# Three blocks on one core: whole-row loads of the key windows, the v-means spread from the load queue, and a new list of steps

## The chip, the core and the metric

The kernel runs on one core of a Trainium2 chip. Its engines work side by side, each through its own list in order: TensorE (PE, with its weight loads PEld), VectorE (DVE), ScalarE (ACT), GpSimd (POOL) and SyncE (SP), which here only issues transfers. The metric is device time in microseconds; of several runs the median counts.

## The reference

Three blocks follow one another. Attention: for 2 batches of 8 heads (768 positions, 64 wide) every query sees the keys within 16 positions and 24 summary keys, each the maximum over a block of 32 keys; the summary values are the means of v over the same blocks.

```
scores_l = scale * np.matmul(q, k.transpose(0, 1, 3, 2))          # kept where |i - j| < 16
scores_s = scale * np.einsum('bhsd,bhnd->bhsn', q, k.reshape(B, H, nb, block, D).max(axis=3)) + np.log(block)
a = softmax(concat([masked scores_l, scores_s]));  out = a @ concat([v, v.mean per block])
```

Then a mixing block: `u = x + (x^T @ U @ V)^T` (rank 32) and `u + relu(u @ w_ch1) @ w_ch2` (512 to 2048 and back), and last a block that shifts by one position: `sigmoid(xr @ w_r) * (relu(xk @ w_k)**2 @ w_v)`. All in float32; the large products run as three products of rounded high and low parts.

## The kernel before, in words

The kernel has a first stage, whose order is written out by hand, and a rest, which is generated by loops. The first stage holds the attention of all eight pairs of heads (numbered 0 to 7; 0 to 3 are batch 0), the rank-32 mixing, and the first quarter of the 2048 hidden units for batch 0. The string ORDER lists its steps by short names; a loop at the end of `build` calls the function of each step, and each step appends its instructions to the engines they belong to. So ORDER sets every engine's own order, and that of the load queue; nothing else moves. Semaphores wait for data and for buffers.

For a pair n of heads, cut into 3 groups g: LK, LQ, LT, LV, LW load keys, queries, v transposed, v in windows (`vcat`), and, for pairs 4 to 7 only, the keys cut into 12 overlapping windows (`kw`, built on GpSimd by KK for pairs 1 to 3). K and SV reduce keys and v by blocks on VectorE, KS writes the 24 block maxima behind each of the 12 windows, SP turns the sums of v on TensorE, VM writes their means from ScalarE, and SPR spreads these means to 12 places in `vcat`. S is the scores (TensorE), X adds the mask (VectorE), E is the exponential (ScalarE), T the transpose (TensorE), C its copy (ScalarE), V the product with the values (TensorE), N the division (VectorE). G, H, U with their copies GC, HC, HS, UC, UL are the rank-32 mixing. F, R, L, Z, Y are the first quarter of the hidden layer. The steps cl, ca, cb, cc, cs, cg, cp, ch, co load a block of weights (two small ones, 0 and 1, then eight of 512 KB) and round it into parts: load; ScalarE (ca, cb); VectorE (cc, cs, cg); GpSimd (cp); ScalarE (ch); GpSimd or VectorE (co).

The raw blocks lie in three staging buffers `stg`, of which blocks 0, 3, 6 and 9 share one: cl9 waits for the step cg6 on VectorE. There are three buffers for keys (`kt`, pair n in n mod 3), three for queries, and two each for `kw`, `vcat` and v transposed. All loads go through the one queue of SyncE; a load that waits for its buffer holds up those behind it. `vcat` has 120 rows of keys, 96 from the window and 24 means, so step V of a pair needs both LV and SPR.

In `spread` (line 208) the means go by GpSimd for pairs 0 to 3, and for 4 to 7 by two transfers, one for each head, issued by ScalarE (line 214). `load_kw` (line 174) writes 96 of each 120 columns of `kw`: 12 pieces of 384 bytes in each of 128 partitions. Behind the first stage come the loads of two small vectors (`muk`, `mur`) and of the next blocks of weights, on the same queue.

Of the kernel before, what the change touches and what calls it, by code (L numbers as in the profile page):

```python
# [42 lines left out]


ORDER = """
LK0 LQ0 cl0 LT0 LK1 LT1 LQ1 cl1 K0 S0.0 S0.1 X0.0 ca0 E0.0 X0.1 TV0.1 S0.2 E0.1 SV0 KK1 LK3 T0.0 K1 TC0.1 SP0
VM0 X0.2 KS1 LK4 E0.2 LK2 SPR0 LQ2 S1.0 LV1 SV1 TV0.2 cb0 TV0.0 X1.0 cb1 T0.1 LT2 TC0.0 S1.2 C0.1 cc1 LT3 S1.1
TC0.2 cg0 V0.1 C0.0 cc0 cs0 cl3 E1.0 KK2 V0.0 K2 SP1 ca1 X1.1 T0.2 cp0 VM1 C0.2 T1.0 X1.2 ch0 KS2 V0.2 SPR1
C1.0 S2.1 N0.0 LV2 E1.2 LK5 LQ3 SV2 KK3 V1.0 E1.1 X2.1 LT4 cl2 T1.2 S2.0 C1.2 N0.2 T1.1 E2.1 N0.1 V1.2 cg1
X2.0 G0 ca3 S2.2 GC0 C1.1 cs1 SP2 T2.1 K3 LW4 E2.0 cp1 LQ4 H0 V1.1 X2.2 VM2 KS3 ch1 LV3 T2.0 HC0 N1.0 C2.1 co1  # L50
S3.1 HS0 E2.2 N1.1 U0.1 SPR2 N1.2 cb2 S3.0 X3.1 C2.0 G1 co0 UC0.1 S3.2 X3.0 E3.0 V2.0 T2.2 SV3 GC1 U0.0 C2.2
X3.2 V2.1 E3.1 V2.2 SV4 SP3 LV4 H1 VM3 cl5 T3.0 ca2 N2.0 SPR3 LQ5 SP4 LT5 N2.1 HC1 C3.0 LW5 T3.1 HS1 E3.2 N2.2
U1.0 cg2 G2 C3.1 cc2 V3.0 cl4 UC0.0 cs2 LQ6 T3.2 VM4 UL0.1 cp2 GC2 U1.1 UC1.0 K4 C3.2 H2 V3.1 HC2 N3.0 YM0
UC1.1 KS4 V3.2 ch2 HS2 UL1.0 U2.0 cb3 co2 S4.1 cb5 N3.2 N3.1 S4.0 SPR4 UL0.0 G3 UL1.1 U2.1 X4.1 F1.0.0 UC2.0
GC3 F1.0.1 E4.1 cg3 F0.0.0 cc3 H3 UC2.1 cs3 F0.0.1 UL2.0 HC3 cp3 ca5 T4.1 HS3 F0.0.2 UL2.1 C4.1 U3.1 X4.0 ch3
U3.0 E4.0 co3 S4.2 SV5 F1.0.2 cb4 X4.2 LT7 T4.0 LK7 ca4 F0.1.0 LT6 C4.0 F0.1.1 cg5 UC3.0 F0.1.2 cc5 cl7 UC3.1
UL3.0 cl6 E4.2 V4.1 LK6 cs5 V4.0 LW6 UL3.1 cp5 LV5 SP5 K5 F0.0.3 VM5 F0.1.3 N4.0 R0.0 KS5 F1.1.0 ch5 N4.1
F1.0.3 SPR5 cg4 F1.1.1 cc4 cl8 co5 S5.0 R1.0 T4.2 L0.0 R0.1 F1.1.2 cs4 cb7 X5.0 F0.2.0 cp4 E5.0 F0.2.1 L1.0
F1.2.0 C4.2 L0.1 F1.2.1 ca7 K6 S5.1 S5.2 cc7 KS6 T5.0 X5.1 E5.1 F1.2.2 F0.2.2 cg7 F1.2.3 C5.0 X5.2 F1.1.3 R1.2
T5.1 R1.1 cs7 V4.2 E5.2 L1.1 cp7 V5.0 N4.2 S6.0 C5.1 L1.2 F0.2.3 ch4 X6.0 T5.2 ch7 co4 G4 C5.2 N5.0 S6.1 ca6  # L60
co7 S6.2 cb6 cg6 V5.1 GC4 E6.0 V5.2 X6.1 cl9 F1.3.0 LV7 E6.1 F1.3.1 LV6 cc6 LQ7 N5.2 F1.3.2 LW7 R0.2 cs6
F0.3.0 SV7 cp6 F0.3.1 F0.3.2 SV6 F0.3.3 ch6 X6.2 F1.3.3 cb8 co6 T6.1 ca8 Z1.0.2 N5.1 C6.1 T6.0 L0.2 SP6 cc8
C6.0 G5 cs8 ca9 SP7 cg8 Z0.0.3 E6.2 K7 Z0.1.3 cp8 Z0.0.2 cb9 Z0.1.2 VM7 Z1.1.2 ch8 cg9 cc9 Z0.0.1 VM6 co8 GC5
cs9 SPR6 Z0.1.1 Z0.0.0 Z0.1.0 KS7 R0.3 H4 cp9 Z0.2.1 R1.3 L0.3 Z0.2.2 L1.3 Z1.2.2 ch9 Z0.2.0 HC4 co9 HS4 S7.1
Z0.2.3 X7.1 Z0.3.3 Z1.3.2 Z0.3.2 Y1.2 H5 Y0.2 Z0.3.1 HC5 E7.1 Y0.3 S7.2 HS5 S7.0 X7.2 SPR7 V6.1 V6.0 Y0.1 T6.2
Z0.3.0 X7.0 U4.1 E7.0 U4.0 N6.0 Z1.0.1 E7.2 N6.1 T7.0 Z1.1.1 UC4.0 Z1.2.1 C6.2 UL4.0 U5.0 C7.0 Y0.0 Z1.3.1
UC5.0 V6.2 V7.0 N6.2 U5.1 UL5.0 T7.1 N7.0 T7.2 C7.1 Y1.1 UC4.1 C7.2 V7.1 V7.2 N7.1 Z1.0.0 N7.2 G6 UL4.1 G7 GC6
Z1.1.0 GC7 H6 Z1.2.0 HC6 UC5.1 H7 HS6 Z1.0.3 HC7 Z1.1.3 HS7 U7.0 U6.0 UC7.0 Z1.2.3 UC6.0 U7.1 UL6.0 Z1.3.0
UL7.0 U6.1 UC6.1 UC7.1 UL6.1 UL7.1 Z1.3.3 Y1.3 UL5.1 Y1.0
"""  # L70
# [808 lines left out]
```

## Time and profile before

| | us |
|---|---|
| median of 3 runs (lowest, highest) | 526.6 (524.32, 528.57) |
| the profiled execution, own time | 525.12 |
| its span | 523.3 |
| PE / DVE / ACT / POOL busy in the span | 505.9 / 319.8 / 250.5 / 195.2 |
| matmuls of the first stage | 5.0 to 114.0 |

The span runs from the first to the last instruction; the 1.8 us around it are start and end. The page's busy time of PE says little about waits by itself, because matmuls overlap and their ends are modelled; the timeline, with the idle time before each instruction, shows them. PEclk is the clock granted to TensorE, as a share of 2.4 GHz. From 114 us on TensorE runs the loops.

### The profile page before, as it was taken

To read this page: it belongs to the slowest core of one execution; us is meant where nothing else is said; L and a number is where in the kernel's file an instruction comes from. 1 tells how busy PE (TensorE), PEld (TensorE's weight loads), DVE (VectorE), ACT (ScalarE), POOL (GpSimd) and SP (SyncE) were. 2 spreads that over 40 slices of the span, in tenths; PEclk is the share of its full clock that TensorE was granted. 3 is DMA by queue.
4 is the path that set the end of the run, shared out by engine and by line. 5 is a ranking of instruction groups with operands and counts; after the bars stand their busy time and mean duration, and the time that the engine had idled before them with its cause. 6 is when DMAs were issued, how large, how long until landed. Compare 5 with 4: busy or idle time off the path is not lost.

```text
span 523.3 us, 8909 instructions
## 1 busy us (share of the span) xinstructions
PE 505.9 (97%) x3468; PEld 469.7 (90%) x3468; DVE 319.8 (61%) x702; ACT 250.5 (48%) x532; POOL 195.2 (37%) x176
## 2 busy tenths in 40 slices
PE   5799989999999999999999999999999999999997
PEld 4578869899999999999999999999879889889885
DVE  5689866646764788738876477556867424443212
ACT  4798676434523545334543445334585534532211
POOL 5544225004653777637776363160622110120000
PEclk9799989999999999999999999999999999999999
DMA  8898939102332333313333150040201001000101
GB/s 293 278 269 267 278 96 249 39 1 81 121 85 76 99 109 117 120 41 120 103 110 110 51 152 3 1 120 5 76 1 60 1 1 60 2 1 20 41 0 60
DMA packets 23737, 48.66 MB, mean 93 GB/s; under 512 B 11264, under 2 KB 11520, under 8 KB 23696
## 3 DMA queue, kind: packets, MB, share of 16 engines
q1 hardware_dynamic: 21120, 47.28, 29.7%
q10 hardware_dynamic: 2544, 0.77, 0.7%
q8 instruction: 27, 0.44, 0.3%
q14 instruction: 14, 0.11, 0.1%
q0 software_dynamic: 32, 0.05, 0.0%
HBM read 44.36 MB, written 3.15 MB: 91 GB/s over the span
## 4 chain that ended last, share of the span: by engine, by line
PE 87%; DMA 4%; ACT 3%; DVE 2%; POOL 1%; issue 1%; SPq 1%; DVEq 0%; POOLq 0%; ACTq 0%
PE bank L511 22%; PE bank L484 22%; PE bank L663 13%; PE bank L685 12%; PE bank L647 5%; DMA kt<-kt 4%; PE bank L579 3%; PE bank L290 2%; PE bank L274 2%; PE bank L555 2%; PE bank L245 2%; PE bank L343 1%; PE bank L312 1%; ACT P L268 1%; PE bank L347 1%
## 5 line engine op out<-in xcount | busy, mean ns | idle before, releaser
L408 POOL TENSOR_TENSOR A<-C,A 128x512 int32<-128x512 int32 (+1 forms) x54 | 70.8, 1311 | 115.9 <-DVE A L402 90.7
L444 POOL TENSOR_TENSOR wlo<-A,whi 128x512 fp32r<-128x512 f32 x50 | 71.1, 1421 | 37.1 <-ACT whi L440 34.7
L511 PE MATMUL bank<-hh,whi 128*128 128x384 f32 x224 | 76.0, 339 | 0.5 <-DVE y L523 0.5
L511 PE MATMUL bank<-hl,whi 128*128 128x384 f32 x224 | 75.7, 338 | 0.0
L511 PE MATMUL bank<-hh,wlo 128*128 128x384 f32 x224 | 75.7, 338 | 0.0
L484 PE MATMUL bank<-uhi,whi 128*128 128x384 f32 x224 | 75.4, 337 | 0.0
L484 PE MATMUL bank<-uhi,wlo 128*128 128x384 f32 x224 | 75.4, 336 | 0.0
L484 PE MATMUL bank<-ulo,whi 128*128 128x384 f32 x224 | 75.4, 336 | 0.0
L491 DVE SCALAR_TENSOR_TENSOR hl<-bank,hh 128x384 fp32r<-128x384 f32 x56 | 31.1, 556 | 68.3 <-ACT hh L489 68.2
L667 DVE TENSOR_TENSOR kt<-kt 128x384 f32<-128x384 f32 x32 | 20.4, 637 | 64.9 <-ACT kt L666 64.8
L385 ACT ACTIVATE A<-stg 128x512 f32<-128x512 uint32 (+1 forms) x54 | 36.3, 673 | 41.9 <-DMA stg<-w 21.6
L489 ACT ACTIVATE hh<-bank 128x384 fp32r<-128x384 f32 x56 | 27.3, 488 | 58.0 <-PE bank L484 57.8
L440 ACT CAST whi<-A 128x512 fp32r<-128x512 f32 x52 | 32.2, 622 | 37.7 <-POOL A L408 37.5
L402 DVE SCALAR_TENSOR_TENSOR A<-stg,A 128x512 int32<-128x512 int32 (+1 forms) x54 | 49.2, 912 | 1.4 <-ACT A L385 1.4
L398 DVE TENSOR_SCALAR C<-C 128x512 int32<-128x512 int32 (+1 forms) x54 | 44.2, 819 | 1.7
L663 PE MATMUL bank<-xkl,whi 128*128 128x384 f32 x128 | 43.2, 338 | 0.6 <-POOL xkl L625 0.6
L511 PEld LDWEIGHTS bank<-hh,whi 128*128 128x128 f32 x224 | 42.0, 188 | 1.5 <-ACT C L388 0.8
L663 PE MATMUL bank<-xkh,whi 128*128 128x384 f32 x128 | 43.2, 337 | 0.0
L663 PE MATMUL bank<-xkh,wlo 128*128 128x384 f32 x128 | 43.1, 337 | 0.0
L484 PEld LDWEIGHTS bank<-ulo,whi 128*128 128x128 f32 x224 | 42.1, 188 | 0.0
L484 PEld LDWEIGHTS bank<-uhi,wlo 128*128 128x128 f32 x224 | 42.1, 188 | 0.0
L511 PEld LDWEIGHTS bank<-hh,wlo 128*128 128x128 f32 x224 | 42.1, 188 | 0.0
(119 smaller groups left out, 1082.6 us busy)
## 6 DMA issues: line engine op xcount, KB each, us to landing
stg<-w SPq DMA_DIRECT2D x32, 512.0 KB, 4.0
stg<-wk SPq DMA_DIRECT2D x8, 512.0 KB, 3.6
stg<-wv SPq DMA_DIRECT2D x8, 512.0 KB, 3.7
vcat<-vw SPq DMA_DIRECT2D x7, 585.0 KB, 10.4
kt<-kt SPq DMA_DIRECT2D x8, 384.0 KB, 6.3
vt<-vt SPq DMA_DIRECT2D x8, 384.0 KB, 6.0
out<-sig SPq DMA_DIRECT2D x12, 256.0 KB, 2.1
qt<-qt SPq DMA_DIRECT2D x7, 384.0 KB, 8.7
```

Of the source, the lines that this page charges most:

```text
L385: nc_s.activation(tmp(i, "A"), st[i]["raw"][:, :, 0].bitcast(U32), AF.Copy, scale=2.0 ** -51, bias=2.0)
L398: nc_v.tensor_scalar(out=c, in0=c, scalar1=3, scalar2=None, op0=ALU.logical_shift_left)
L402: nc_v.scalar_tensor_tensor(out=a, in0=st[i]["raw"][:, :, 1], scalar=-2 ** 31, in1=a, op0=ALU.bitwise_and, op1=ALU.bitwise_or)
L408: nc_p.tensor_tensor(out=a, in0=c, in1=a, op=ALU.add)
L440: nc_s.copy(wt[key][0], w)
L444: eng.tensor_tensor(out=lo, in0=w, in1=hi.bitcast(F32), op=ALU.subtract)
L484: nc_t.matmul(ps, w[:, sl], x[:, k], start=(n == 0), stop=(n == 3 * KD - 1))
L489: nc_s.activation(hh, ps, AF.Relu)
L491: lambda: nc_v.scalar_tensor_tensor(out=hl, in0=ps, scalar=0.0, in1=hh.bitcast(F32), op0=ALU.max, op1=ALU.subtract)
L511: nc_t.matmul(acc[d], w[:, sl], x, start=(i == 0 and n == 0), stop=(i == FT - 1 and n == 2))
L663: nc_t.matmul(ps, w[:, sl], x[:, k], start=(n == 0), stop=(n == 3 * KD - 1))
L685: nc_t.matmul(acc, x[:, sl], w, start=(f == 0 and n == 0), stop=(f == KFT - 1 and n == 2))
```

## The change

`kw` of batch 1 is loaded with its full width of 120 columns: the array in memory gets 24 columns of zeros behind each window, and each partition is one piece of 5760 bytes. KS writes the maxima over these zeros, and so now waits for the load. The means of v get a third dimension with a column of ones (filled once), so that the 130 values of a place in `vcat` are written in one run; for pairs 4 to 7 SPR is one transfer, and SyncE issues it, in the queue of the loads. ORDER is a new list of the same 526 steps. The rest is unchanged.

```
 ORDER = """
-LK0 LQ0 cl0 LT0 LK1 LT1 LQ1 cl1 K0 S0.0 S0.1 X0.0 ca0 E0.0 X0.1 TV0.1 S0.2 E0.1 SV0 KK1 LK3 T0.0 K1 TC0.1 SP0
...
+LK0 LQ0 LK1 LT0 cl0 K0 S0.0 X0.0 S0.1 TV0.0 S0.2 E0.0 T0.0 TV0.1 TV0.2 X0.1 K1 X0.2 SV0 LK2 K2 E0.1 ca0 cb0
...
+SV1 S1.1 S1.0 S1.2 X1.0 T0.2 V0.0 V0.1 SP1 ca1 cb1 E1.0 cc0 X1.1 cg1 N0.0 cs0 C0.2 VM1 E1.1 N0.1 X1.2 E1.2 SV2
...
+    vm_b = [a_p.tile([128, 2, D + 1], F32, name=f"vm{i}", bufs=1) for i in range(2)]
+    for vc, vm in zip(vcat, vm_b):
...
+        nc_p.memset(vm[KW:KC], 1.0)
...
     def load_kw(n):
-        nc.sync.dma_start(out=kw_b[n % 2][:, :, 0:KW], in_=I["kw"][n - 4])
+        nc.sync.dma_start(out=kw_b[n % 2], in_=I["kw"][n - 4])
...
     def v_mean(n):
         held = ps_t.pop(("SP", n))
-        vm = vm_t[n] = a_p.tile([128, 2, D], F32, name="vm", bufs=2)
         nc_s.activation(
-            vm[KW:KC].rearrange("p h d -> p (h d)"), held[0][KW:KC, 0:2 * D], AF.Copy, scale=1.0 / BLK
+            vm_b[n % 2][KW:KC, :, 0:D], held[0][KW:KC, 0:2 * D].rearrange("p (h d) -> p h d", h=2), AF.Copy,
+            scale=1.0 / BLK,
         )
...
     def spread(n):
-        src = vm_t.pop(n)[KW:KC].unsqueeze(1).to_broadcast([NB, NT, 2, D])
+        src = vm_b[n % 2][KW:KC].rearrange("p h d -> p (h d)").unsqueeze(1).to_broadcast([NB, NT, 2 * (D + 1)])
+        dst = vcat[n % 2][KW:KC].rearrange("p t h d -> p t (h d)")
         if n < 4:
-            nc_p.tensor_copy(vcat[n % 2][KW:KC, :, :, 0:D], src)
+            nc_p.tensor_copy(dst, src)
         else:
-            for h in range(2):
-                nc_s.dma_start(out=vcat[n % 2][KW:KC, :, h, 0:D], in_=src[:, :, h])
+            nc.sync.dma_start(out=dst, in_=src)
...
-    ar["kw"] = kp[:, :, win]
+    ar["kw"] = np.concatenate([kp[:, :, win], np.zeros((4, 2 * D, NT, NB), np.float32)], axis=-1)
```

Three places show how the list moves work. The first is the load queue (SyncE) from its fourth transfer on; kt_110, kt_111 and kt_112 are the three key buffers, so kt_112 takes the keys of pair 2. Before, and then in the change:

```order
L376 DMA stg<-uva 128x1024
L169 DMA vt_113<-vt 128x768
L159 DMA kt_111<-kt 128x768
L169 DMA vt_114<-vt 128x768
L166 DMA qt<-qt 128x768
L376 DMA stg<-vb 96x896
L159 DMA kt_110<-kt 128x768
L159 DMA kt_111<-kt 128x768
L159 DMA kt_112<-kt 128x768
L166 DMA qt<-qt 128x768
L172 DMA vcat_105<-vw 96x1560
```

```order
L161 DMA kt_111<-kt 128x768
L171 DMA vt_113<-vt 128x768
L378 DMA stg<-uva 128x1024
L161 DMA kt_112<-kt 128x768
L171 DMA vt_114<-vt 128x768
L168 DMA qt<-qt 128x768 x2
L378 DMA stg<-vb 96x896
L168 DMA qt<-qt 128x768
```

The keys of pair 2 were the twelfth transfer, behind the keys of pairs 3 and 4; they are now the seventh.

The second is the same queue further on, around the loads for pair 5: its window of values is the first `vcat_105<-vw` below, and `vcat<-vm` is a spread of means. Before, and then in the change:

```order
L159 DMA kt_111<-kt 128x768
L169 DMA vt_113<-vt 128x768
L376 DMA stg<-w 128x1024 x2
L159 DMA kt_110<-kt 128x768
L175 DMA kw_108<-kw 128x12x96
L172 DMA vcat_105<-vw 96x1560
L376 DMA stg<-w 128x1024 x2
L172 DMA vcat_105<-vw 96x1560
```

```order
L177 DMA kw_109<-kw 128x1440
L174 DMA vcat_105<-vw 96x1560
L216 DMA vcat_104<-vm_125 24x12x130
L174 DMA vcat_104<-vw 96x1560
L161 DMA kt_111<-kt 128x768
L177 DMA kw_108<-kw 128x1440
L378 DMA stg<-w 128x1024
L161 DMA kt_110<-kt 128x768
L171 DMA vt_113<-vt 128x768
L171 DMA vt_114<-vt 128x768
L177 DMA kw_109<-kw 128x1440
L216 DMA vcat_105<-vm_126 24x12x130
```

The values of pair 5 stood behind the keys and windows of pair 6 (kt_110, kw_108) and two blocks of weights; they now stand ahead of all of pair 6. The spread of pair 5 (the last row) stands in this queue, behind the windows of keys of pair 7 (the second kw_109).

The third is ScalarE in pair 5. L268 before and L270 in the change are exponentials, L279 and L281 the copies C, L385 and L387 the first step on a block of weights (ca). Before, and then in the change:

```order
L562 ACTIVATE hh_1202<-bank_1132 128x384
L562 ACTIVATE hh_1210<-bank_1062 128x384
L268 ACTIVATE P<-P,nm 128x120 x4
L279 COPY pt_106<-bank_1205 120x512
L440 CAST whi<-A 128x512 x2
L279 COPY pt_107<-bank_1265 120x512
L385 ACTIVATE A<-stg 128x512
L388 ACTIVATE C<-stg 128x512
L317 COPY g_1321<-bank_1274 128x128
```

```order
L270 ACTIVATE P<-P,nm 128x120 x4
L442 CAST whi<-A 128x512
L387 ACTIVATE A<-stg 128x512
L281 COPY pt_107<-bank_1314 120x512
L442 CAST whi<-A 128x512
L390 ACTIVATE C<-stg 128x512 x2
L270 ACTIVATE P<-P,nm 128x120 x4
L387 ACTIVATE A<-stg 128x512
```

In the change the first step on weight block 8 stands between the exponentials of the last group of pair 5 and the copy that its product V5.2 waits for; the first exponentials of pair 6 follow behind. Before, it came after that copy.

## Rows read from the trace of the kernel before

**Rows 1.** Stretches: span, busy PE, PEld, DVE, ACT, POOL (counts), PEclk, DMA share, GB/s.

```profile
21.10:27.20 6.10, 6.07 (x73) 4.72 (x73) 4.72 (x26) 4.27 (x13) 3.97 (x5) 0.52 0.71 212
45.00:50.00 5.00, 5.00 (x66) 4.53 (x66) 4.81 (x19) 3.45 (x11) 1.79 (x2) 1.00 1.12 334
67.90:70.40 2.50, 0.00 (x0) 0.01 (x1) 1.54 (x4) 2.50 (x8) 1.54 (x2) 1.00 0.37 113
70.40:77.00 6.60, 6.58 (x116) 5.19 (x116) 3.80 (x21) 3.14 (x10) 0.99 (x1) 0.74 0.07 8
...
114.00:523.30 409.30, 404.35 (x2161) 383.20 (x2159) 240.53 (x375) 175.03 (x331) 155.34 (x120) 1.00 0.20 62
```

**Rows 2.** Timeline of TensorE: start, us, instruction, count, [idle before, releaser].

```profile
18.17 0.65 PE L274 MATMUL bank<-ident,P 128*120 128x128 f32 x4
21.13 1.08 PE L274 MATMUL bank<-ident,P 128*120 128x128 f32 x4 [2.31 <-DVE nm L257]
...
63.07 1.05 PE L245 MATMUL bank<-kw,qt 64*64 64x120 f32 x32
...
67.18 0.69 PE L290 MATMUL bank<-vcat,pt 121*64 121x65 f32 x16
70.42 0.69 PE L290 MATMUL bank<-vcat,pt 121*64 121x65 f32 x16 [2.56 <-ACT whi L440]
...
75.84 1.15 PE L290 MATMUL bank<-vcat,pt 121*64 121x65 f32 x32
```

**Rows 3.** Timeline of VectorE around two reductions of keys.

```profile
19.43 0.95 DVE L180 TENSOR_REDUCE ks<-kt 128x24 f32<-128x768 f32 x1 [2.50 <-DMA kt<-kt]
...
63.91 0.95 DVE L180 TENSOR_REDUCE ks<-kt 128x24 f32<-128x768 f32 x1 [1.90 <-DMA kt<-kt]
```

**Rows 4.** Timeline of the load queue on SyncE, transfers issued.

```profile
10.55 1.33 SPq L159 DMA_DIRECT2D kt<-kt  x3
...
29.66 0.65 SPq L175 DMA_DIRECT2D kw<-kw  x1
30.36 1.91 SPq L166 DMA_DIRECT2D qt<-qt  x1
...
55.36 0.55 SPq L175 DMA_DIRECT2D kw<-kw  x1
55.95 4.31 SPq L172 DMA_DIRECT2D vcat<-vw  x1
60.37 15.94 SPq L376 DMA_DIRECT2D stg<-w  x2
77.04 0.80 SPq L172 DMA_DIRECT2D vcat<-vw  x2
...
78.98 3.98 SPq L787 DMA_DIRECT2D muk<-moe_mu_k  x1
```

**Rows 5.** Timeline of ScalarE, with the issues of its own queue (ACTq).

```profile
13.94 1.17 ACT L388 ACTIVATE C<-stg 128x512 f32<-128x512 f32 x2
...
23.09 2.40 ACT L268 ACTIVATE P<-P,nm 128x120 f32<-128x120 f32 x8
...
45.12 1.41 ACTq L214 DMA_DIRECT2D vcat<-vm  x1
...
46.58 0.79 ACTq L214 DMA_DIRECT2D vcat<-vm  x1
...
68.96 0.57 ACT L279 COPY pt<-bank 120x512 f32<-120x512 f32 x1
```

**Rows 6.** DMA issues by tile: queue, count, size of one, median us to landing.

```profile
vcat<-vw SPq DMA_DIRECT2D x7, 585.0 KB, 10.4
...
kw<-kw SPq DMA_DIRECT2D x4, 576.0 KB, 8.7
```

**Rows 7.** Landing times of the weight blocks in the first stage (tile view).

```profile
DMA to landing us min/median/max: 4.3/5.8/11.1
```

**Rows 8.** Timeline of GpSimd: one spread of head pair 0.

```profile
12.88 1.47 POOL L211 COPY vcat<-vm 24x1536 f32<-24x1536 f32 x1 [1.79 <-ACT vm L203]
```

More of the change, by code (lines that the diff above doesn't have):

```diff
@@ L45 @@
 ORDER = """
-LK0 LQ0 cl0 LT0 LK1 LT1 LQ1 cl1 K0 S0.0 S0.1 X0.0 ca0 E0.0 X0.1 TV0.1 S0.2 E0.1 SV0 KK1 LK3 T0.0 K1 TC0.1 SP0
[L47 to L69, printed above, removed]
+LK0 LQ0 LK1 LT0 cl0 K0 S0.0 X0.0 S0.1 TV0.0 S0.2 E0.0 T0.0 TV0.1 TV0.2 X0.1 K1 X0.2 SV0 LK2 K2 E0.1 ca0 cb0
+TC0.0 T0.1 SP0 TC0.1 E0.2 VM0 C0.1 C0.0 TC0.2 KK1 KK2 KS1 LT1 LQ1 LQ3 cl1 LQ2 LV1 LT2 cl2 cl3 LK3 KS2 SPR0 cg0
@@ new lines @@
+SV1 S1.1 S1.0 S1.2 X1.0 T0.2 V0.0 V0.1 SP1 ca1 cb1 E1.0 cc0 X1.1 cg1 N0.0 cs0 C0.2 VM1 E1.1 N0.1 X1.2 E1.2 SV2
+cp0 SPR1 YM0 KK3 V0.2 N0.2 S2.0 T1.0 C1.0 T1.1 S2.1 X2.1 C1.1 T1.2 V1.0 SP2 S2.2 X2.0 K3 X2.2 E2.1 C1.2 ch0
+E2.0 VM2 KS3 G0 V1.1 V1.2 T2.1 T2.0 S3.0 cb2 ca2 GC0 SPR2 C2.0 N1.0 N1.1 N1.2 cc1 cs1 G1 H0 LV2 LW4 LT3 LK4
+LV3 LT4 cl5 LK5 V2.0 X3.0 E2.2 GC1 HC0 C2.1 T2.2 cp1 co0 C2.2 ch1 co1 HS0 SV3 E3.0 S3.2 S3.1 cc2 X3.1 H1 SP3
+VM3 E3.1 U0.1 U0.0 V2.1 V2.2 UC0.1 HC1 UC0.0 cg2 cs2 cp2 SPR3 X3.2 N2.0 HS1 N2.2 N2.1 UL0.1 SV4 T3.0 T3.1 E3.2
@@ new lines @@
+C3.0 ch2 U1.0 T3.2 G2 V3.0 U1.1 C3.1 UC1.0 cb3 GC2 ca3 C3.2 UC1.1 co2 cb5 K4 UL1.0 UL0.0 N3.0 cg3 SP4 F1.0.0
+V3.1 VM4 H2 V3.2 HC2 cc3 cs3 N3.2 HS2 N3.1 UL1.1 KS4 cl7 LQ4 S4.0 F0.0.0 F0.0.1 S4.1 X4.0 LT5 cp3 ch3 co3 cl6
+LQ5 LQ6 LW5 LV5 SPR4 LV4 LK7 G3 GC3 cb7 X4.1 U2.0 F1.0.1 H3 HC3 UC2.0 U2.1 HS3 F1.1.0 U3.1 U3.0 UL2.0 F0.1.0
+F0.1.1 UC2.1 ca5 UC3.1 E4.0 UC3.0 UL2.1 cc5 SV5 cg5 cs5 UL3.1 S4.2 F0.0.2 X4.2 UL3.0 cc7 cs7 cp5 E4.1 ca7
+F1.0.2 F1.1.1 F1.1.2 T4.0 F1.0.3 T4.1 F1.1.3 E4.2 R1.0 C4.0 ch5 F0.0.3 F0.1.2 T4.2 F0.1.3 C4.1 R1.1 cg7 K5 co5
@@ new lines @@
+R0.0 KS5 S5.0 L1.0 L1.1 L0.0 SP5 cp7 cb6 ca6 VM5 X5.0 V4.0 V4.1 C4.2 S5.1 S5.2 V4.2 N4.0 N4.1 X5.1 cg6 ch7 co7
+LW6 cl4 LK6 LT6 LT7 LW7 SPR5 LQ7 cl9 cl8 LV6 F1.2.0 F0.2.0 F0.2.1 F0.2.2 F1.3.0 F1.2.1 R0.1 L0.1 F1.2.2 F0.2.3
+cb4 ca4 cg4 E5.1 E5.0 T5.0 F1.3.1 R0.2 C5.0 T5.1 F1.2.3 F1.3.2 K6 cc6 X5.2 N4.2 cc4 cs4 cs6 C5.1 R1.2 E5.2
+L0.2 KS6 S6.0 X6.0 cp4 ch4 ca8 cp6 co4 S6.1 V5.0 V5.1 T5.2 F0.3.0 F0.3.1 F0.3.2 C5.2 ch6 co6 V5.2 N5.0 N5.1
+SV6 X6.1 N5.2 L1.2 cb8 cb9 E6.0 ca9 cc8 cc9 cg8 S6.2 SP6 G4 G5 VM6 cs8 cs9 cg9 GC5 GC4 E6.1 cp8 ch8 F0.3.3
@@ new lines @@
+R0.3 co8 cp9 ch9 co9 Z0.0.3 Z0.1.3 F1.3.3 R1.3 X6.2 K7 Z1.0.1 Z1.1.1 Z0.0.0 Z0.1.0 L0.3 T6.1 Z0.0.1 Z0.1.1
+Z0.0.2 Z0.1.2 Z0.2.3 Z0.2.2 Z1.2.1 Z0.2.0 T6.0 C6.1 L1.3 Z1.3.1 Y1.1 SV7 H4 H5 Z0.3.2 Z0.3.3 Y0.2 Y0.3 E6.2
+C6.0 HC4 HC5 HS4 Z0.2.1 Z0.3.1 SP7 Y0.1 HS5 VM7 KS7 LV7 SPR6 SPR7 S7.2 X7.2 S7.1 S7.0 E7.2 X7.1 X7.0 E7.1 E7.0
+V6.0 V6.1 T6.2 Z0.3.0 Y0.0 N6.0 U4.1 U4.0 U5.0 T7.0 T7.2 T7.1 C6.2 V6.2 UC4.0 UL4.0 C7.0 V7.0 UC5.0 C7.1 C7.2
+N6.2 Z1.0.3 Z1.1.3 U5.1 Z1.2.3 V7.2 V7.1 UL5.0 N7.0 N7.2 N6.1 N7.1 Z1.0.0 Z1.1.0 G6 G7 Z1.2.0 GC7 GC6 H7 H6
@@ L70 @@
+HC7 HC6 HS7 HS6 Z1.0.2 Z1.3.0 Z1.1.2 U6.0 Z1.2.2 U7.0 Z1.3.3 Y1.0 UC6.0 UL6.0 Z1.3.2 U7.1 UC4.1 UC7.0 UL7.0
+UC7.1 UC5.1 UL5.1 Y1.2 UL4.1 U6.1 UL7.1 Y1.3 UC6.1 UL6.1
 """
@@ L151, in build @@
         eng.memset(t[:, WIN + S:], 0.0)
-    for vc in vcat:
+    vm_b = [a_p.tile([128, 2, D + 1], F32, name=f"vm{i}", bufs=1) for i in range(2)]
+    for vc, vm in zip(vcat, vm_b):
         nc_p.memset(vc[KW:KC + 1], 0.0)
         nc_p.memset(vc[:, :, :, D:D + 1], 1.0)
-    ks_t, vs_t, vm_t, q_t, s_t, p_t, pt_t, o_t, x_t, g_t, u_t, y_t, ps_t = ({} for _ in range(13))
+        nc_p.memset(vm[KW:KC], 1.0)
+    ks_t, vs_t, q_t, s_t, p_t, pt_t, o_t, x_t, g_t, u_t, y_t, ps_t = ({} for _ in range(12))
     def load_k(n):
```

## The prediction, made before the changed kernel had run

> **What bounds the kernel now.** I read the stretches first, then TensorE's timeline for its waits, then for each wait the timelines of the engine and the queue that ended it. From 114.0 us to the end TensorE is busy for 404.4 of 409.3 us [rows 1]. The loops there are not edited and hold three quarters of the time, so the change can act only before 114.0. There TensorE sits idle for long in three places: 5.0 us for the first load, 2.31 us up to 21.13, and 2.56 us up to 70.42 [rows 2]. The last two are followed by stretches in which the granted clock is 0.52 over 6.1 us and 0.74 over 6.6 us, so largely the 1.2 GHz level in place of 2.4 [rows 1].
>
> The wait at 21.13 begins with the keys of pair 2. SyncE issues three key loads at 10.55, and pair 2 is the last of them [rows 4]; VectorE sits 2.50 us until it lands at 19.4, reduces it, and only then reaches the masks that TensorE needs [rows 3]. The wait at 70.42 is the product V5.0. The profile names a cast on ScalarE, but the copy that V5.0 needs starts at 68.96 and takes 0.57 us [rows 5], so something later ended it. Its window of values is issued at 55.95 by an instruction that holds SyncE for 4.31 us, right behind the windows of keys in 12 pieces per partition [rows 4]. The last row issued in that backlog before the queue stalls is a weight block; blocks of this stage take up to 11.1 us to land [rows 7]. I read it as the values landing at about 70.
>
> **The first wait.** It costs 2.31 us, and the slow stretch behind it 6.1 x (1 - 0.52) = 2.9 us, together 5.2. In the change pair 2's keys are the seventh transfer and wait for no buffer, so by their place they land at about 10 us and not at 19.4; the reduction K2 stands ahead of the masks of pair 1 and does not hold them. New short gaps come: the copy C0.2 now stands behind two conversions (1.17 for two, [rows 5]) and four exponentials (half of 2.40, [rows 5]), and product V0.2 waits for it; the copy of U that G0 needs stands behind 28 exponentials (8.4 us at 0.30) and some 20 other short ScalarE operations. Walking those rows I get about 1 us each. The give-back lies between 0 and 5.2 (a gap long enough to bring the slow clock back); I take 2.0, net **-3.2**.
>
> **The second wait.** It costs 2.56 us and 6.6 x (1 - 0.74) = 1.7 us, together 4.3. In the change pair 5's values stand ahead of everything for pair 6, and windows of keys in 128 pieces, not 1536, should no longer hold the next issue for 1.91 to 4.31 us as in [rows 4]. What is late next: weight blocks 8 and 9 now come behind all of pairs 6 and 7's keys, and ScalarE meets block 8 earlier (below). Between 0 and 4.3 comes back; I take 1.0, because the last block needs to land only by about 70, net **-3.3**.
>
> **The other edits.** The four pairs of issues that leave ScalarE took 2.20 us for the first pair (1.41 and 0.79, [rows 5]). TensorE showed no wait for ScalarE there, so I cost it at 0 and keep the bound of -2 for the first two pairs. SyncE takes over four issues of below 1 us. The GpSimd spreads stay at 1.47 us [rows 8], 24x1560 in place of 24x1536: 0. The wider windows add 4 x 0.144 = 0.6 MB, at 334 GB/s [rows 1] 1.8 us of transfers, if fewer pieces save nothing; the earlier order of loads hides them, and if it did not they would cost those 1.8. KS now waits for its windows: these are issued some ten transfers before their pair's keys are reduced, and only GpSimd's conversions stand behind KS; 0, at most 1. The two small vectors now sit behind the spread of pair 7, so are issued near 85 and not at 78.98, and hold the queue for some 8 us (3.98 each, [rows 4]); the weight blocks behind them are still out by 95, before the loops begin: 0.
>
> **The sum.** 525.1 (the profiled execution's own time) - 3.2 - 3.3 = 518.6. That execution lies 1.5 under the median of 526.6; the same gain from the median gives 520.1. I predict **519.5**, with 514 to 522 as this case's own range. Within 1% of 526.6, about what this kernel's measurement can tell from no change, is 521.3 to 531.9.
>
> **Rival: the second wait stays and only changes its cause.** V5.0 also needs the spread of pair 5. It used to go out on ScalarE's queue, and now stands in the load queue behind the 720 KB of windows of pair 7, which wait for the last scores of pair 5. These end at 64.1 before [rows 2], so at about 61 now. V5.0 is reached at about 68: 70.4 less the wait 2.56 and the first gain 3.2, plus some 3 us of hidden-layer products that now stand ahead of it. A spread that takes 6 us lands in time; one that takes the 10.4 of a window of values [rows 6] lands at 71 to 72, and brings back 3 us and a slow stretch of 1.7. That gives 518.6 + 4.3 = 523. For it: the transfers ahead; against it: little is queued by then.
>
> The Trainium skill's page "DMA: Bandwidth & Descriptors", section "Queues, rings and completion order", speaks against the move: each DMA engine takes turns between the queue rows that have work, and works through one row in order. By that rule a spread on ScalarE's row takes turns with the loads, and one on the loads' row waits for the whole backlog; the sum would be this rival's 523. No row above shows two queues in turn.
>
> **Rival, slower: ScalarE is caught behind weight block 8.** Its first step now stands ahead of the copy for V5.2 and of all exponentials of pair 6. The block's load stands behind cl9, which waits for the shared staging buffer until VectorE has done cg6. This happened before: two weight loads fill 60.37 to 76.3, with four window and query loads behind [rows 4]. There it cost nothing, because ScalarE met that block late. TensorE comes to V5.2 at 76.4 before [rows 2], at about 70 now. Every microsecond by which block 8 lands after 70 is lost. If the pair is issued only at 76.3 and takes the median 5.8 [rows 7], it lands at 82: 12 us of waiting and 3 of slow clock, 518.6 + 15 = 533.6. Against it: cg6 moved forward, from behind N5.0 to right behind X5.1, so I expect it near 59.
>
> **Rival: only one gain holds,** since transfers, VectorE and ScalarE are all close to full between 30 and 60 us (VectorE 4.81 of 5.00 in [rows 1]) and what TensorE gains early it waits for later: 525.1 - 3 = 522. **Rival: more comes,** both waits vanish without give-back, and the relief of ScalarE counts: 525.1 - 9.5 - 2 = 513.6.
>
> **How the numbers follow.** Forecast 0.45, the spread in the queue 0.16, one gain 0.15, more 0.09, slower 0.15. The forecast lies under 521.3 in about nine parts of ten, the 523 and 522 cases in a third; with the 0.09 that makes 0.58 for faster. The slower case passes 531.9 in most of its chance: 0.13. The rest, 0.29, is within 1%. The range 512 to 530 takes in the first four cases with their bounds, and a mild form of the slow one.
>
> **What would show it.** Pair 2's keys reduced before 13 us, and no idle above 1.5 us on TensorE between 14 and 30: the first term. V5.0 without a wait, and the instruction behind each windows load shorter than 1 us on SyncE: the second. The matmuls of the loops starting at about 107.5 and not at 114.0, then the same 409.3 us: that nothing else matters. Wrong would be: a wait of TensorE above 2 us between 50 and 75 with ScalarE waiting for a weight block, or a spread landing last before V5.0; or a loop stretch that is not 409 us.

## The result

| | median, us (lowest to highest, runs) | against before, 95% interval |
|---|---|---|
| before | 526.66 (524.32 to 528.57, 4) | |
| changed | 520.47 (519.29 to 521.79, 4) | 0.9885 (0.9839 to 0.9932) |
| changed, a second time | 523.10 (519.67 to 526.02, 12) | 0.9955 (0.9929 to 0.9980) |

The first comparison is the result that the forecast is held against: 6.2 us faster, forecast 519.5. The second, from a later set of runs with 23 of before, is 2.4 us (0.0045 of 525); the two intervals barely meet. The change makes the kernel faster: the two comparisons say 2.4 and 6.2 us, and their intervals reach from 1 to 8.5. A gain of 7, as I forecast, is at the far end of that.

The profiled execution of the changed kernel took 521.79, the longest of the four; its span is 519.7. Its stretches (columns as in [rows 1]):

```profile
21.50:27.20 5.70, 5.23 (x94) 3.80 (x96) 3.46 (x20) 4.08 (x13) 0.85 (x3) 1.00 0.53 162
...
70.00:77.00 7.00, 4.61 (x87) 3.95 (x85) 3.91 (x23) 3.32 (x7) 3.48 (x4) 1.00 0.64 186
...
4.96:110.19 105.23, 96.99 (x1308) 84.40 (x1309) 78.71 (x322) 73.82 (x200) 36.78 (x40) 1.00 0.70 217
...
110.20:519.70 409.50, 404.44 (x2161) 383.39 (x2160) 240.07 (x376) 175.60 (x332) 155.32 (x120) 1.00 0.20 62
```

And one stretch of before, from the first matmul to the first one of the loops, to be held against the third row above:

```profile
4.99:113.98 108.99, 101.52 (x1308) 86.50 (x1309) 77.76 (x323) 74.12 (x201) 35.74 (x39) 0.95 0.70 203
```

The last row of the changed kernel answers to the last of [rows 1]: 409.5 us of loops against 409.3, so nothing changed there. The gain is all in the first stage: 105.23 us against 108.99. The 1308 matmuls are the same. The busy time fell by 4.5 us (101.52 to 96.99), at a clock of 1.00 in place of 0.95: the two slow stretches of before, which I had put at 2.9 and 1.7, are not there (first and second row: a clock of 1.00). **The idle time did not fall in this pair:** 108.99 - 101.52 = 7.5 before, 105.23 - 96.99 = 8.2 after.

A second profile of each kernel, from the later set (before, then changed), divides the gain otherwise:

```profile
5.61:115.65 110.04, 100.66 (x1308) 85.39 (x1309) 77.52 (x323) 74.04 (x201) 35.05 (x39) 0.98 0.72 201
...
5.59:108.48 102.89, 97.38 (x1309) 84.73 (x1309) 78.29 (x322) 73.70 (x200) 36.15 (x40) 1.00 0.70 220
```

Here the first stage is 7.2 us shorter, 3.3 of it in the busy time and 3.9 in the idle time (9.4 to 5.5). So how the gain divides into clock and waiting differs from execution to execution; that it lies before the loops does not.

TensorE's timeline in the first profile of the changed kernel shows where the idle time is (columns as in [rows 2]):

```profile
19.18 0.68 PE L292 MATMUL bank<-vcat,pt 121*64 121x65 f32 x14 [0.99 <-ACT pt L281]
21.55 0.33 PE L292 MATMUL bank<-vcat,pt 121*64 121x65 f32 x2 [1.69 <-issue]
...
60.61 1.05 PE L247 MATMUL bank<-kw,qt 64*64 64x120 f32 x32
...
70.04 1.15 PE L292 MATMUL bank<-vcat,pt 121*64 121x65 f32 x32
...
75.76 0.69 PE L292 MATMUL bank<-vcat,pt 121*64 121x65 f32 x16 [2.39 <-ACT pt L281]
```

V5.0 (70.04) starts without a wait. But 0.99 and 1.69 us are idle around V0.2, and 2.39 before V5.2. The last scores of pair 5 start at 60.61 and not at 63.07 [rows 2]. VectorE reduces pair 2's keys at 12.68, not at 19.43 [rows 3]:

```profile
12.68 0.94 DVE L182 TENSOR_REDUCE ks<-kt 128x24 f32<-128x768 f32 x1
```

SyncE shows the load queue (issues only, as in [rows 4]). Behind the windows of keys of pair 7 (61.79) the next transfer goes out at once, where one took 4.31 us before; the spread of pair 5 follows at 62.21, and weight block 8 is the second of the pair at 63.74. The instructions behind all four windows in this profile took 0.38 to 0.84 us:

```profile
61.79 0.33 SPq L177 DMA_DIRECT2D kw<-kw  x1
62.21 0.84 SPq L216 DMA_DIRECT2D vcat<-vm  x1
...
63.74 1.20 SPq L378 DMA_DIRECT2D stg<-w  x2
...
79.40 0.83 SPq L216 DMA_DIRECT2D vcat<-vm  x1
...
91.26 0.78 SPq L216 DMA_DIRECT2D vcat<-vm  x1
```

The chain of waits (start, us, what ended the wait) and ScalarE's timeline name the wait before V5.2. Block 8 needs 9.98 us from issue to landing; ScalarE stands 3.63 us in front of its first step (74.58), and the copy for V5.2 stands behind that step (75.14):

```profile
64.51 9.98 DMA stg<-w
```

```profile
74.58 0.66 ACT L387 ACTIVATE A<-stg 128x512 f32<-128x512 uint32 x1 [3.63 <-DMA stg<-w]
75.14 0.57 ACT L281 COPY pt<-bank 120x512 f32<-120x512 f32 x1
```

### The profile page after: what moved, and what is told of

Same layout as the page of the kernel before. It is cut to its first block, busy times and chain, and to the rows that moved or that the text cites. A ratio compares the mean times of both kernels' runs of the same rounds, so it can differ in the third digit from the quotient of the medians.

```text
span 519.7 us, 8914 instructions
## 1 busy us (share of the span) xinstructions
PE 501.4 (96%) x3468; PEld 467.8 (90%) x3468; DVE 320.4 (62%) x702; ACT 250.7 (48%) x532; POOL 196.1 (38%) x178
## 4 chain that ended last, share of the span: by engine, by line
PE 84%; DMA 6%; ACT 4%; DVE 2%; issue 2%; POOL 1%; SPq 0%; ACTq 0%; DVEq 0%; POOLq 0%
PE bank L513 21%; PE bank L486 21%; PE bank L665 13%; PE bank L687 12%; PE bank L649 5%; DMA stg<-w 5%; PE bank L581 3%; PE bank L292 2%; PE bank L557 2%; PE bank L276 2%; PE bank L247 1%; DMA vt<-vt 1%; PE bank L345 1%; ACT pt L281 1%; ACT P L270 1%
## 5 line engine op out<-in xcount | busy, mean ns | idle before, releaser
L387 ACT ACTIVATE A<-stg 128x512 f32<-128x512 uint32 (+1 forms) x54 | 36.3, 672 | 40.3 <-DMA stg<-w 24.7
L486 PEld LDWEIGHTS bank<-uhi,whi 128*128 128x128 f32 x224 | 42.1, 188 | 0.0
```

The lines of the kernel that those rows point to most:

```text
L387: nc_s.activation(tmp(i, "A"), st[i]["raw"][:, :, 0].bitcast(U32), AF.Copy, scale=2.0 ** -51, bias=2.0)
L486: nc_t.matmul(ps, w[:, sl], x[:, k], start=(n == 0), stop=(n == 3 * KD - 1))
```

## The experiments

Each is compared with runs of the kernel before on the same chip in the same set (35, 26 and 23 runs; medians 525.3, 525.2 and 524.9, set by set: four kernels, then four, then the last four rows). The ratio compares the runs of one set with each other and can differ a little from the quotient of the two medians (0.9972 in the first row); gains against before in us are taken from the ratio. The changed kernel itself ran in the last set only, so what is measured against it in the second set is given by both of its comparisons. "First stage" is the profiled execution from the first matmul to the loops, with TensorE's idle time in it and the granted clock.

| kernel | median, us (runs) | against before, 95% interval | first stage, idle, clock |
|---|---|---|---|
| old list, both edits | 523.8 (12) | 0.9962 (0.9932 to 0.9991) | 106.3, 7.6, 1.00 |
| new list, no edits | 528.6 (12) | 1.0044 (1.0013 to 1.0074) | 111.6, 10.7, 0.95 |
| before, pair 2's keys early | 522.6 (12) | 0.9948 (0.9920 to 0.9977) | 108.8, 9.1, 0.98 |
| before, pair 5's values early | 522.8 (12) | 0.9945 (0.9914 to 0.9976) | 105.3, 7.0, 1.00 |
| changed, ca8 later | 520.6 (9) | 0.9900 (0.9869 to 0.9932) | 101.7, 4.2, 1.00 |
| changed, old windows | 523.2 (12) | 0.9958 (0.9928 to 0.9987) | 107.4, 7.5, 0.97 |
| changed, spreads on ScalarE | 524.4 (12) | 0.9985 (0.9955 to 1.0014) | 107.7, 9.3, 0.98 |
| old list, two moves, both edits | 520.2 (6) | 0.9902 (0.9864 to 0.9940) | 103.4, 4.2, 1.00 |
| before again | 526.85 (1) | | 110.0, 9.4, 0.98 |
| changed again | 523.1 (12) | 0.9955 (0.9929 to 0.9980) | 102.9, 5.5, 1.00 |
| changed, three moves | 521.4 (6) | 0.9910 (0.9876 to 0.9944) | 103.5, 5.4, 1.00 |
| changed, last two spreads on ScalarE | 526.2 (12) | 1.0016 (0.9987 to 1.0044) | 109.0, 9.0, 0.97 |

### The edits without the list, and the list without the edits

The changed kernel with the ORDER of before:

> The changed kernel with the list of steps of before: only the two edits of transfers are left (windows of keys as one piece per partition, spread as one transfer on the load queue). Theory A (the list removes two waits, the edits are worth little): the wait of 2.3 us at about 21 stays with its slow stretch; the wait before V5.0 may shrink, because the windows no longer hold the queue; 0 to -2 us against before. Theory B (the edits carry the gain: fewer pieces, ScalarE relieved of its issues): -4 to -6 us, all of the difference between the two kernels.

The kernel before with the ORDER of the change:

> The kernel before with the new list of steps and nothing else: windows of keys in 12 pieces, two spreads per pair on ScalarE's queue. Theory A: -4 to -6 us against before, as the change itself; both waits (at 21 and before V5.0) gone. Theory B: within 1.5 us of before, with new waits behind the windows of keys in the load queue or behind the issues on ScalarE.

The edits alone gain 0.4% (2.0 us; 0.5 to 3.6), at the upper end of what theory A gave them. But the wait of 2.3 us at about 21 that it expected to stay is not in this profile: there are 0.94 and 0.91 us near 20 and 22, and the clock from 21 to 27 is 1.00. The wait before V5.0, in TensorE's timeline of this kernel, is down to 0.66 us:

```profile
68.35 0.69 PE L292 MATMUL bank<-vcat,pt 121*64 121x65 f32 x16 [0.66 <-ACT P L270]
```

The list alone **loses** 0.4% (2.3 us; 0.7 to 3.9). Theory B had new waits of this kind, at no more than 1.5 us. TensorE's timeline of the second kernel shows three waits, and ScalarE's the causes of the last two:

```profile
34.74 0.38 PE L198 MATMUL bank<-ident,vs 128*24 128x128 f32 x2 [2.40 <-DVE vs L194]
...
78.41 1.14 PE L290 MATMUL bank<-vcat,pt 121*64 121x65 f32 x16 [3.08 <-ACT pt L279]
...
98.91 0.34 PE L290 MATMUL bank<-vcat,pt 121*64 121x65 f32 x4 [1.47 <-DMA vcat<-vm]
```

```profile
77.23 0.66 ACT L385 ACTIVATE A<-stg 128x512 f32<-128x512 uint32 x1 [4.48 <-DMA stg<-w]
...
81.75 0.27 ACT L203 ACTIVATE vm<-bank 24x128 f32<-24x128 f32 x1
...
96.08 3.36 ACTq L214 DMA_DIRECT2D vcat<-vm  x4
```

At 34.74 the reduction of pair 3's values is late, at 78.41 block 8 (ScalarE waits 4.48 us for it), and at 98.91, in V6.0, the spread of the means of pair 6: they are written at 81.75, but their spread goes out only from 96.08 on, together with that of pair 7 and right behind VM7 (96.07). So list and edits don't add up (+2.3 and -2.0 against -2.4 to -6.2 together): the list needs the edits.

### The two terms of the sum, one move each

```diff
-... SV0 KK1 LK3 ... KS1 LK4 E0.2 LK2 SPR0
+... SV0 KK1 LK2 LK3 ... KS1 LK4 E0.2 SPR0
```

> The kernel before with one load moved: the keys of pair 2 ahead of those of pairs 3 and 4. Theory A, first term: the wait of 2.31 us at 21.13 and its slow stretch (2.9 us) go, some of it comes back: -3.2 us against before (-1 to -5.2). Rival (the time gained early is only waited for later, at the next place where transfers, VectorE or ScalarE are late): the wait at 21 goes, but the score matmuls of pair 5 start as late as before, and the time is within 1 us of before.

```diff
-... X4.2 LT7 T4.0 LK7 ... UL3.1 cp5 LV5 SP5
+... X4.2 LV5 LT7 T4.0 LK7 ... UL3.1 cp5 SP5
```

> The kernel before with one load moved: the window of values of pair 5 ahead of the last loads for pairs 6 and 7 that stand before it. Theory A, second term: V5.0 waits for these values; the wait of 2.56 us at 70.42 and its slow stretch (1.7) go: -3.3 us against before (0 to -4.3). Rival 1: V5.0 waits for something else (the spread of the means, or ScalarE): the wait stays, within 0.5 us of before. Rival 2: the wait moves to the next product (V5.2) or to pair 6 and the time is within 1 us.

Both gain half a per cent: 2.7 us (1.2 to 4.2) and 2.9 (1.3 to 4.5). The second is shown in its trace too: V4.2 and V5.0 are one run of 32 products, with no wait between:

```profile
67.69 1.15 PE L290 MATMUL bank<-vcat,pt 121*64 121x65 f32 x32
```

The first shows less plainly. In the profiled execution, the slowest of its twelve (525.49), V5.0 still waits, and 2.15 us are lost in the middle of V2.2, where the trace names nothing that TensorE waited for (the last section comes back to it):

```profile
38.56 0.46 PE L290 MATMUL bank<-vcat,pt 121*64 121x65 f32 x9 [2.15 <-issue]
...
70.86 0.69 PE L290 MATMUL bank<-vcat,pt 121*64 121x65 f32 x16 [2.02 <-ACT whi L440]
```

A fixed point behind it is the first scores of pair 4; here, and in the old list with two moves and both edits (in the table), which has this move too:

```profile
45.91 1.35 PE L245 MATMUL bank<-kw,qt 64*64 64x120 f32 x32
```

```profile
43.27 1.31 PE L247 MATMUL bank<-kw,qt 64*64 64x120 f32 x32
```

Counted from the first matmul that is 40.3 and 37.4 us. The first profile has 2.9 us in two stops of this kind (0.76 and 2.15), the second 0.36; without them it would be 37.4 and 37.0. The four profiles with the old order of pair 2's keys have 39.0 to 40.0, or 38.2 to 40.0 without such stops. So some 1 to 3 us are gained by there, an estimate from single profiles.

### Was the first wait there at all?

The kernel before, profiled once more.

> The kernel before once more, for a second profile. The traces of two kernels whose list is that of before up to 40 us showed pair 2's keys reduced at 18.0 and 18.2 and a wait of 0.9 us near 20, at the full clock; the profile that I predicted from showed 19.43, 2.31 us and a stretch at 0.52. Theory A (the first wait is a matter of when the transfers of one execution land): K2 at about 18, a wait of about 1 us, no slow stretch behind it, and the loops start some 2 to 4 us before 114.0 unless V5.0 loses more. Rival (the kernel before always has it): 2 us or more at about 21 and a clock of 0.5 to 0.7 behind it. The wait before V5.0 should show in either case, 2 to 3 us.

TensorE's and VectorE's timelines and one stretch of this second execution:

```profile
22.07 0.69 PE L290 MATMUL bank<-vcat,pt 121*64 121x65 f32 x16 [0.70 <-POOL vcat L211]
...
30.90 0.64 PE L245 MATMUL bank<-kw,qt 64*64 64x120 f32 x16 [1.48 <-DMA qt<-qt]
...
45.26 1.34 PE L245 MATMUL bank<-kw,qt 64*64 64x120 f32 x32
...
72.14 0.69 PE L290 MATMUL bank<-vcat,pt 121*64 121x65 f32 x16 [3.37 <-ACT whi L440]
```

```profile
17.56 0.95 DVE L180 TENSOR_REDUCE ks<-kt 128x24 f32<-128x768 f32 x1 [0.48 <-DMA kt<-kt]
```

```profile
21.00:27.00 6.00, 4.76 (x102) 3.40 (x94) 4.25 (x23) 4.93 (x16) 2.28 (x3) 1.00 1.04 280
```

The keys of pair 2 are reduced at 17.56, there is no wait above 0.7 us near 21, and the clock is 1.00. Yet the scores of pair 4 start at 45.26, and in the execution from which I predicted, with its 2.31 us and the stretch at 0.52, they start no later:

```profile
44.99 1.31 PE L245 MATMUL bank<-kw,qt 64*64 64x120 f32 x32
```

Counted from the first matmul (4.99 and 5.61) that is 40.0 us and 39.7. The two other profiles with the old order of these keys (both edits; pair 5's values early) have no long wait near 21 either, and are there at 39.7 and 39.0. So the 5.2 us of the first term belonged to one execution, and by 45 us it is only 0.3 to 1.0 behind the executions without them: these lose time elsewhere, the second one 1.48 us on a load of queries at 30.90 and 0.91 in a stop at 37.90. The wait before V5.0 is there in both, 2.56 and 3.37. Theory A holds for the wait, but its loops do not start earlier (115.65): V5.0 lost more.

### The two edits inside the new list

```diff
-        nc.sync.dma_start(out=kw_b[n % 2], in_=I["kw"][n - 4])
+        nc.sync.dma_start(out=kw_b[n % 2][:, :, 0:KW], in_=I["kw"][n - 4])
```

> The changed kernel with the windows of keys loaded as before, in 12 pieces of 384 bytes per partition; the spread stays on the load queue. The new list alone measured 2.3 us slower than before, the edits alone 2 faster, both together 6 faster. Theory A (the windows are the edit that the new list needs: 12 pieces make the transfers behind them land late, block 8 first of all): 3 to 7 us slower than the changed kernel, with ScalarE's wait for block 8 longer than 3.63 us. Rival (the spread is that edit, or ScalarE's relief): within 1 us of the changed kernel.

```diff
-            nc.sync.dma_start(out=dst, in_=src)
+            nc_s.dma_start(out=dst, in_=src)
```

> The changed kernel with its one spread transfer issued by ScalarE, on ScalarE's own queue. My sum costs that part of the change at nothing: within 1 us of the changed kernel. Rival 1 (a queue of its own lets the spread pass the backlog of loads, the rule of the Trainium skill's page named in the prediction): V5.0 and V6.0 get their means earlier; since nothing waits for them now, no gain, but spreads that land sooner. Rival 2 (ScalarE is short of time and of room in the fifties: 4 issues of about 1 us): 1 to 3 us slower.

```diff
-            nc.sync.dma_start(out=dst, in_=src)
+            (nc.sync if n < 6 else nc_s).dma_start(out=dst, in_=src)
```

> The changed kernel with the spreads of pairs 6 and 7 alone issued by ScalarE; those of pairs 4 and 5 stay on the load queue. With all four on ScalarE the kernel lost about 4 us; its trace shows ScalarE issuing two for 1.65 us at 90.4, the exponentials of pair 7 behind them, and TensorE waiting 2.00 us for these with a stretch at 0.83 behind. Theory A (that place is the price): 2.5 to 4 us slower than the changed kernel. Rival (the price is in the forties and fifties, at pairs 4 and 5): within 1 us of the changed kernel.

The old windows: the load queue is held again, 6.11 us right behind one window (issued at 51.88) and 3.61 us three transfers behind another (44.66), and V4.0 waits 2.91 us for its values:

```profile
47.11 3.61 SPq L174 DMA_DIRECT2D vcat<-vw  x1
...
52.55 6.11 SPq L378 DMA_DIRECT2D stg<-w  x1
```

```profile
61.87 1.43 PE L292 MATMUL bank<-vcat,pt 121*64 121x65 f32 x21 [2.91 <-DMA vcat<-vw]
```

In time that is 0.9958 of before; against the 0.9885 and 0.9955 of the change, a loss of nothing to 3.8 us. The direction of the windows' part is in the trace; its size is not settled. Theory A's sign did not come: ScalarE waits 2.78 us for block 8, not more than 3.63, and V5.2 waits 1.37.

The spreads on ScalarE: 524.4, a loss of 1.6 to 5.3 by the same two comparisons, and more than the 1 us that I had as my own theory. The trace says how, and it is none of the three. ScalarE's and TensorE's timelines:

```profile
78.56 0.27 ACT L204 ACTIVATE vm<-bank 24x128 f32<-24x128 f32 x1
...
90.39 0.27 ACT L204 ACTIVATE vm<-bank 24x128 f32<-24x128 f32 x1 [2.19 <-PE bank L200]
90.40 1.65 ACTq L216 DMA_DIRECT2D vcat<-vm  x2
```

```profile
93.77 1.39 PE L292 MATMUL bank<-vcat,pt 121*64 121x65 f32 x32 [2.00 <-ACT P L270]
```

The means of pair 6 are written at 78.56, but both spreads go out from 90.40 on. In the new list the steps SPR6 and SPR7 stand together behind VM7, and on ScalarE a transfer waits in line like any step, here until VM7 has run, 12 us later. On SyncE nothing stands between: in the changed kernel the same means are written at 79.11 and spread at 79.40 (the queue's rows above), and only the second spread waits for VM7, until 91.26:

```profile
79.11 0.27 ACT L204 ACTIVATE vm<-bank 24x128 f32<-24x128 f32 x1
...
90.97 0.27 ACT L204 ACTIVATE vm<-bank 24x128 f32<-24x128 f32 x1 [2.19 <-PE bank L200]
```

V6.0 follows the scores of pair 7 at 93.77, with 2.00 us of idle time (the row names an exponential that ends later; V6.0 needs the spread issued at 90.40, and in the list without the edits, above, where the spreads also stand behind VM7, the row of the same product names the spread), and the stretch from 90 to 100 us runs at 0.83. With the last two spreads alone on ScalarE the same is seen,

```profile
91.45 2.27 ACTq L216 DMA_DIRECT2D vcat<-vm  x2
```

```profile
94.97 1.33 PE L292 MATMUL bank<-vcat,pt 121*64 121x65 f32 x30 [2.14 <-ACT P L270]
```

and the loss against the changed kernel in the same set is 3.1 us (526.2 against 523.1; 1.4 to 4.6 from the scatter of the 12 runs of each). It lies within the 1.6 to 5.3 of all four, so these two can be the whole price; it is theory A's number, by another mechanism than the issue time that it named.

On the queues themselves: pair 5's spread in this kernel was issued at 59.84 on ScalarE's own queue and its packets moved from 62 to 66 us, beside the loads (queue, packets, MB, share of the 16 engines, from 63 to 66):

```profile
q1 hardware_dynamic: 107, 0.48, 79.9%
q10 hardware_dynamic: 185, 0.09, 26.4%
```

In the changed kernel it was issued at 62.21 behind the windows of pair 7, and its small packets moved from 66 to 68. Both needed about 6 us. The Trainium skill's page "DMA: Bandwidth & Descriptors", section "Queues, rings and completion order", has the engines take turns between rows; these rows agree, but the turn brought the means no sooner, and V5.0 at 70.04 had them either way.

### The step behind block 8, and a better list

```diff
-L0.2 KS6 S6.0 X6.0 cp4 ch4 ca8 cp6 co4 ... N5.2 L1.2 cb8 cb9 E6.0
+L0.2 KS6 S6.0 X6.0 cp4 ch4 cp6 co4 ... N5.2 L1.2 ca8 cb8 cb9 E6.0
```

> The changed kernel with one step moved: the first step on weight block 8 (ca8) goes behind the copy and the product V5.2, to right before the next step on that block. In the changed kernel ScalarE sits 3.63 us on that block and TensorE 2.39 us before V5.2. Theory A (that wait is lost time, the small form of the slower rival): V5.2 waits for nothing, -2 us against the changed kernel (0 to -2.4), about 518.5. Rival (the block is late anyway, and what follows V5.2 needs it, or the next thing late takes its place): the wait moves to pair 6's exponentials or to the products of the hidden layer, within 0.7 us of the changed kernel.

The copy for V5.2 is now ahead of block 8 on ScalarE, and V5.2 has no wait:

```profile
70.45 0.59 ACT L281 COPY pt<-bank 120x512 f32<-120x512 f32 x1 [0.87 <-PE bank L276]
...
72.97 0.70 ACT L387 ACTIVATE A<-stg 128x512 f32<-128x512 uint32 x1 [1.41 <-DMA stg<-w]
```

```profile
71.94 0.69 PE L292 MATMUL bank<-vcat,pt 121*64 121x65 f32 x16
```

This profile has the shortest first stage of all, 101.72 us with 4.2 idle. The time is 0.9900 of before, between the two comparisons of the changed kernel: from a loss of 0.8 us to a gain of 2.9. That the wait goes is shown, what it is worth is not.

```diff
-... SP1 ca1 cb1 E1.0 ... cs0 C0.2 VM1 ... E1.2 SV2 cp0 ... X2.1 C1.1 T1.2 V1.0 SP2 S2.2 ... C1.2 ch0
+... SP1 ca1 C0.2 cb1 E1.0 ... cs0 VM1 ... E1.2 cp0 ... X2.1 SV2 C1.1 T1.2 V1.0 S2.2 ... C1.2 SP2 ch0
```

The next two ran in one set: the changed kernel unedited, and with this edit and the one above.

> The changed kernel once more, to be compared with the next two on the same chip: about 520.5 us, 0.988 to 0.992 of before. Theory A of the step behind block 8: its profile shows the 2.4 us before V5.2 again, with ScalarE 3 to 4 us on that block. Of the 1.69 us inside V0.2, for which the trace names no cause: a matter of the execution, 0 to 2 us here.

> The changed kernel with three places of the list mended: ca8 behind V5.2 (2.39 us of TensorE's idle time); the copy C0.2 ahead of the second conversion of block 1 and of the exponentials of pair 1 (0.99 us before V0.2); the reduction SV2 and its turn SP2 behind the masks of pair 2's second group (VectorE sits 2.12 us on the transposed values of pair 2 ahead of the masks). Theory A (idle time of TensorE before the loops is lost time): the three waits go, -2 to -4 us against the changed kernel in the same runs. Rival (the starts of the first stage are set by transfers, and what one wait loses the next gives back): within 1 us of it.

The changed kernel shows the same wait before V5.2 as the first time, 2.72 us, with ScalarE 3.97 us on block 8, and nothing in the middle of V0.2. Its time, 523.1 and 0.9955 of before, is outside what I expected of it.

```profile
74.05 0.69 PE L292 MATMUL bank<-vcat,pt 121*64 121x65 f32 x16 [2.72 <-ACT pt L281]
```

With the three moves no wait before V5.2 is left, but V4.0 now waits for the window of values of pair 4:

```profile
60.00 1.15 PE L292 MATMUL bank<-vcat,pt 121*64 121x65 f32 x32 [2.53 <-DMA vcat<-vw]
```

521.4 against 523.1, 1.7 us less; from the scatter of 6 and 12 runs the difference of the means, 2.1, is uncertain by 1.6. It is the better version of the two if that holds, though its profile has no shorter first stage (103.5 against 102.9); both theories get a part.

The old list with the two moves above and both edits:

> The changed kernel with the list of before in which only two loads are moved: the keys of pair 2 ahead of those of pairs 3 and 4, the values of pair 5 ahead of the last loads for pairs 6 and 7. Theory A (the two waits and the two edits are all there is, the rest of the new list is worth nothing): within 1 us of the changed kernel. Rival (other moves of the new list matter too): 1.5 to 3.5 us slower than the changed kernel, as the old list with both edits.

It took 520.2, 0.9902 of before, with 4.2 us idle. It is as fast as the changed kernel within what these comparisons tell, so two moved loads and the two edits are enough; nothing else in the new list had to be there.

## Why the prediction was right, and where it was not

- **The sum.** 518.6 from the profiled execution, 519.5 as the forecast; 520.5 came, and 523.1 the second time. Inside the range, but by terms of another size than mine.
- **The first wait, -3.2.** The move does what I said, and alone it gained 2.7 us. But I read its price from a single execution. The second profile of before has neither the 2.31 us nor the slow stretch, and is at the same place by 45 us: the give-back, which I took as 2.0 of 5.2, was 4.2 or more in the execution that I had. That the sum came out near the result here is in part luck; what the move gains shows only in later starts, some 1 to 3 us by 45, and not as the wait that I priced. And "no idle above 1.5 us between 14 and 30" failed once, with the stop of 1.69 us in V0.2, and held the second time.
- **The second wait, -3.3.** Right in cause: the move of these values alone takes it away and gains 2.9 us, and the two edits with the old list leave 0.66 of 2.56. The instructions behind the windows are below 1 us, as said. The give-back, 1.0, was too small: 2.39 to 2.72 us came back at V5.2.
- **"The other edits" at 0.** This failed. With the old list they gain 2.0 us together, and the new list without them is slower than before. Of the two, the spreads' part is shown inside the new list (3.1 us for those of pairs 6 and 7); the windows' part is open, between nothing and 3.8. I bounded ScalarE's relief by the issue time of the first pair, -2. I did not ask where SPR6 stands on its engine: for the spread, not the time of an issue counts but what it is queued behind.
- **Slower, ScalarE behind weight block 8.** The mechanism came, as written, at a fifth of the waiting (2.39 of 12 us). It is also the first sign that I named for being wrong, a wait of TensorE above 2 us with ScalarE waiting for a weight block: 2.39 us up to 75.76, and 2.72 up to 74.05 the second time. The block was issued at 64.51, not at 76.3, because cg6 did come early, but not near 59 either: cg6 ran at 62.52, and the windows of pair 7 ahead in the queue waited for pair 5's last scores until 61.79. It took 9.98 us, not the median 5.8, and landed at 74.5, not 82. I gave it all or nothing; a mild form belonged in the likeliest case.
- **The spread late in the load queue.** Did not come: 6 us, in time for V5.0.
- **The loops.** 409.5 us, as said; they start at 110.2 and 108.5 in the two profiles, where I had 107.5.

## What to carry to other kernels

A wait seen in one profile of a kernel whose runs scatter by 1% may belong to that execution; take a second profile, or look whether the next fixed point is later too, before it enters a sum. A transfer's place is set by the list of the engine that issues it: ask what stands ahead of it there, not only how long the issue takes. When loads are moved ahead of others, look for the step that meets the ones moved back, and keep it behind what the critical engine waits for.
